# A transformer block on one core: an opening in a written order, query heads parted by DMA, and a planner that waits for copies

## The chip, the core and the metric

The kernel runs on one core of a Trainium2 chip. A core has five engines that run side by side and each take their instructions strictly in order: TensorE (PE, matrix products into PSUM), VectorE (DVE), ScalarE (ACT, here mostly exponentials), GpSimd (POOL) and SyncE (SP, which here only issues DMAs). PSUM has eight banks of 128 x 512 fp32 values. The metric is the device time of one execution in microseconds; smaller is better.

## The reference

One block of a transformer over 2048 tokens of width 512, with 32 heads of width 16 and a gated feed-forward layer of width 1792, in bfloat16:

```python
qkv = layernorm(x) @ wqkv                       # split into q, k, v: 32 heads of 16
p   = softmax(q @ k.T * 16 ** -0.5)             # per head, 2048 x 2048
h   = x + (p @ v) @ wo
g, u = layernorm(h) @ w_gate, layernorm(h) @ w_up
out = h + (sigmoid(g) * u) @ w_down
```

All 2048 x 2048 scores of each of 32 heads must be exponentiated. That is most of the work: 2048 units of 128 keys x 512 queries.

## The kernel before, in words

**Heads and tiles.** Keys lie transposed in `KT[p]`, 128 rows for eight heads of 16 rows each. A score product uses 32 rows (two heads) at a time, so that four row groups j work side by side in the array. To get one head out of two, the queries are kept twice: in `QT[2p]` the rows of the odd heads are zero, in `QT[2p+1]` those of the even heads. `mask` (128 x 2) has the ones and zeros for this, `maskz` the same times the scale of the scores. `QTb` is a second home for the first pair of chunk 1. A group g is one of the eight `QT` tiles: four heads, one for each j.

**Exponentials on two engines.** Scores fall into PSUM tiles of two or three units (L1110). ACT exponentiates most units (L1475, `pt`, `xnT`, `xb`, `pe`, `QTb` are only different homes of its results). DVE takes the other units by integer arithmetic on the bits of fp16 numbers: one pass out of PSUM (L1292), then two shifted copies of it, made mostly by GpSimd (L1313). The value product (L1268) then has three parts for such a unit in place of one, or two where DVE adds two of the parts first (L1337).

**Value products.** `Vaug` has per head 16 value columns and one column of 0.5, which gives the sum of the softmax; `Vaug2` is a weighted copy. The sums gather in PSUM bank 0 (`acc`), which must be cleared before its first use.

**The opening** (L200 to L515). `x` comes in four chunks of 512 rows; chunk 0 is loaded row tile by row tile (128 rows each). The path to the first scores is, per row tile i: statistics (`s`), with a correction (`f`) where ACT computed them, root (`q`), reciprocal (`r`), normalization (`a`), transpose on PE (`t`), copy out of PSUM (`e`), and products with the first 128 columns of the key and query weights (`p`, `w`=0 or 1). Then keys are copied to `KT[0]` (`kt`) and queries to `QT[0]` and `QT[1]` (`qt`, `qu`), in halves of 256 columns. A small list scheduler (L449 to L512) chooses at build time which of these tasks goes next on which engine, by a rank and by assumed times; `go` marks that the first scores may start. Matmuls on a constant tile keep PE warm meanwhile (`keep_warm`, L475). Constants (a ramp, the identity, the masks, the 0.5 columns) are made by GpSimd, DVE and ACT between these tasks.

**The planner.** After the opening, one long loop (L1394 on) walks over score tiles and writes the instructions of all engines in an order of its own. It keeps a clock per engine (`T`), assumed costs for each kind of work, and queues of jobs for DVE, ACT and GpSimd. Dense products (projections, output projection, the feed-forward layer of finished query chunks) and value products fill PE between score tiles; if nothing fits, `stir` (L678) issues a matmul whose result isn't used. `PLAN` is a table of a few hundred overrides found offline: the key 16n + step changes what PE does at a step of tile n, and steps 12, 14 and 15 steer whether DVE adds parts, which j DVE takes, and whether DVE takes a unit of this tile at all. Since each override shifts the clocks, all later decisions depend on it.

**The query projection** (`prep_q`, L768). Four dense products, one scaling copy out of PSUM into `qd` (L778), and then two `split_q` instructions on DVE (L327) which multiply `qd` by the two columns of `mask` into the two `QT` tiles. It runs 15 times: for each pair p of each chunk, without the first one that the opening does itself. All DMAs after the opening (feed-forward weights at L855, transposes of normalized rows at L593 and L837, residual rows, outputs) are issued by SyncE in the order in which the planner reaches them.

Of the kernel before, what the change touches and what calls it, by code (L numbers as in the profile page):

```python
# [22 lines left out]
PLAN = {176: 5, 239: 2, 367: 1, 383: 1, 414: 3, 432: 9, 480: 5, 492: 1, 496: 3, 512: 4, 561: 1, 592: 3, 593: 9, 606: 3, 609: 3, 736: 5, 751: 2, 780: 2, 785: 1, 796: 1, 800: 4, 831: 1, 844: 2, 849: 3, 894: 3, 897: 9, 914: 9, 928: 3, 960: 2, 976: 3, 1025: 2, 1040: 3, 1041: 5, 1052: 2, 1072: 3, 1088: 2, 1100: 2, 1104: 5, 1105: 3, 1120: 3, 1170: 1, 1233: 3, 1280: 3, 1328: 4, 1359: 2, 1392: 3, 1440: 2, 1486: 3, 1681: 1, 1824: 5, 1840: 9, 1872: 4, 1953: 3, 1982: 1, 2001: 3, 2080: 3, 2095: 2, 2129: 3, 2161: 3, 2162: 2, 2176: 4, 2222: 1, 2239: 2, 2256: 4, 2257: 9, 2274: 4, 2287: 2, 2350: 3, 2412: 1, 2430: 2, 2465: 9, 2479: 2, 2480: 9, 2512: 2, 2556: 2, 2560: 4, 2574: 2, 2588: 2, 2592: 5, 2608: 9, 2767: 1, 2818: 3, 2833: 9, 2849: 5, 2864: 3, 2908: 1, 2972: 2, 3020: 1, 3036: 1, 3056: 1, 3072: 3, 3169: 4, 3180: 2, 3184: 4, 3217: 2, 3234: 4, 3280: 4, 3360: 2, 3537: 2, 3617: 3, 3644: 2, 3681: 9, 3744: 3, 3756: 2, 3760: 3, 3820: 2, 3905: 4, 3938: 3, 3953: 3, 4066: 4, 4080: 3, 4081: 4, 4096: 2, 4112: 2, 4124: 1, 4129: 9, 4191: 2, 4204: 1, 4207: 2, 4225: 3, 4268: 2, 4284: 1, 4288: 2, 4337: 2, 4352: 3, 4398: 3, 4510: 2, 4526: 1, 4641: 4, 4700: 2, 4734: 3, 4737: 4, 4752: 9, 4754: 2, 4784: 4, 4802: 4, 4878: 3, 4880: 4, 4910: 2, 4924: 1, 4928: 1, 4930: 4, 5022: 2, 5058: 3, 5072: 4, 5090: 3, 5121: 4, 5164: 1, 5182: 3, 5185: 3, 5200: 3, 5201: 3, 5265: 4, 5280: 3, 5294: 1, 5308: 1, 5345: 2, 5359: 1, 5360: 9, 5378: 3, 5388: 1, 5424: 1, 5471: 1, 5488: 1, 5522: 2, 5553: 3, 5566: 3, 5600: 2, 5633: 4, 5650: 9, 5696: 2, 5712: 4, 5728: 4, 5742: 2, 5756: 2, 5760: 3, 5840: 2, 5906: 1, 5938: 3, 6082: 9, 6095: 2, 6096: 2, 6108: 2, 6140: 1, 6192: 3, 6194: 9, 6268: 1, 6274: 3, 6289: 4, 6319: 1, 6337: 5, 6384: 1, 6431: 2, 6432: 4, 6463: 2, 6464: 4, 6528: 3, 6544: 3, 6592: 1, 6607: 2, 6624: 1, 6641: 2, 6656: 2, 6687: 2, 6689: 9, 6753: 9, 6799: 1, 6832: 2, 6847: 2, 6865: 1, 6929: 2, 6972: 2, 6974: 1, 7024: 1, 7040: 3, 7106: 9, 7152: 5, 7154: 9, 7244: 2, 7248: 3, 7281: 3, 7296: 2, 7312: 1, 7376: 2, 7408: 9, 7410: 2, 7468: 1, 7504: 4, 7505: 2, 7520: 3, 7535: 2, 7553: 4, 7566: 3, 7570: 4, 7585: 3, 7596: 2, 7676: 1, 7681: 5, 7695: 2, 7728: 4, 7776: 3, 7793: 2, 7839: 2, 7852: 1, 7886: 2, 8016: 2, 8033: 2, 8063: 2, 8128: 2, 8209: 4, 8257: 9, 8290: 4, 8305: 9, 8338: 4, 8382: 2, 8432: 5, 8494: 3, 8529: 5, 8591: 2, 8609: 5, 8626: 2, 8706: 3, 8721: 4, 8768: 4, 8800: 4, 8848: 2, 8849: 5, 8860: 1, 8863: 2, 8881: 3, 8882: 4, 8895: 2, 8896: 3, 8897: 2, 8910: 3, 8927: 1, 8946: 4, 8961: 4, 9006: 1, 9024: 3, 9026: 9, 9054: 3, 9073: 2, 9116: 2, 9120: 3, 9137: 4, 9153: 2, 9249: 5, 9276: 2, 9358: 2, 9376: 3, 9377: 9, 9407: 1, 9408: 1, 9426: 9, 9457: 3, 9504: 2, 9518: 3, 9520: 4, 9584: 9, 9586: 4, 9600: 2, 9678: 1, 9697: 1, 9711: 2, 9727: 2, 9728: 1, 9762: 9, 9776: 4, 9792: 4, 9841: 9, 9854: 2, 9855: 2, 9857: 9, 9872: 3, 9900: 1, 9919: 2, 9932: 1, 9964: 2, 9968: 3, 10028: 2, 10032: 2, 10044: 2, 10047: 1, 10146: 2, 10160: 5, 10172: 1, 10176: 3, 10177: 3, 10210: 4, 10273: 4, 10284: 1, 10304: 3, 10334: 1, 10364: 2, 10380: 2, 10417: 9, 10433: 4, 10464: 1, 10556: 1, 10622: 1, 10624: 4, 10626: 9, 10636: 1, 10640: 4, 10690: 3, 10702: 2, 10705: 3, 10734: 3, 10754: 4, 10801: 3, 10802: 2, 10816: 2, 10848: 9, 10912: 1, 10913: 1}  # L23
# [121 lines left out]
def kernel(  # L145
# [103 lines left out]
    nc.vector.memset(eps_t[:], 1e-5)  # L249
    nc.scalar.activation(out=A0[:], in_=eps_t[:], func=ACT.Sqrt)  # L250
# [3 lines left out]
    nc.gpsimd.memset(power[:], -0.5)  # L254
    ramp = prep.tile([P, 2, 32], BF16, name="ramp")
    for k in range(32):
        nc.gpsimd.memset(ramp[:, 0, k:k + 1], float(k))
# [6 lines left out]
    def halves():  # L264
        nc.scalar.activation(out=Vaug[:, :, :, DH:VW], in_=fill[:].rearrange("p (t h o) -> p t h o", t=NT, o=1),
                             func=ACT.Copy, scale=0.5)

    def masks():
        nc.vector.tensor_reduce(out=mask[:], in_=ident_bf[:].rearrange("p (b a d) -> p a b d", a=2, d=DH),
                                axis=AX.XY, op=ALU.max)  # L270
        nc.vector.tensor_scalar(out=maskz[:], in0=mask[:], scalar1=ZS, scalar2=None, op0=ALU.mult)

# [57 lines left out]
    psp = main.enter_context(tc.tile_pool(name="psum", bufs=1, space=PSUM))  # L330
    PS = psp.tile([P, 8, QC], FP32, name="PS")
    free_banks = [5, 7, 6, 3, 2, 1, 0]
    held_banks = {}

    def bank0(key):
        b = held_banks[key] = free_banks.pop()
        return PS[:, b, :]

    def free0(key):
        free_banks.append(held_banks.pop(key))  # L340
# [7 lines left out]
    class Task:  # L348
        def __init__(self, name, deps, opts, bank=0, frees=0):
            self.name, self.deps, self.opts, self.bank, self.frees = name, deps, opts, bank, frees  # L350
            self.end = None
            tasks[name] = self

    def fixed(name, at):
        Task(name, [], []).end = at

    V, A, E = nc.vector, nc.scalar, nc.tensor

    ACT_STATS = {(0, 1)}

    def stats_task(c, i):
        src, mv = xb[c][:, i, :], mvs[c][:, i, :]

        def on_act():
# [6 lines left out]
        Task(("s", c, i), [("x", c, i)], [("A", 1650, on_act)] if (c, i) in ACT_STATS  # L371
             else [("D", 870, lambda: ln_stats(src, mv))])
        Task(("f", c, i), [("s", c, i)], [("D", 300, lambda: fix(c, i))] if (c, i) in ACT_STATS
             else [("N", 0, lambda: None)])
# [19 lines left out]
    def copy0(c, i, eng):  # L394
        eng(out=xnv[c][:, i], in_=buf["t", c, i])
        free0(("t", i))
# [7 lines left out]
    def keys0(half, act):  # L404
        cs = slice(half * 2 * P, (half + 1) * 2 * P)
        (A.copy if act else V.tensor_copy)(out=KT[0][:, cs], in_=buf[0][:, cs])
        if half:
            free0(0)

    def query0(half, a, act=False):  # L410
        cs = slice(half * 2 * P, (half + 1) * 2 * P)
# [5 lines left out]
        if half and a:  # L417
            free0(1)

    fixed("w0", 5000.0)  # L420
    for c in range(NQC):
        for i in range(TQ):
            fixed(("x", c, i), (3150.0 + 450 * (i // 2)) if c == 0 else 4800.0 + 2100 * c + 150 * i)
            stats_task(c, i)
# [1284 lines left out]
```

## Time and profile before

The median of three runs is 734.85 us (734.73 to 734.94); the profiled execution spans 733.3 us, and the clock granted to TensorE was 0.999 of full speed.

| what | busy us | share |
|---|---|---|
| PE | 712.8 | 97% |
| ACT | 703.1 | 96% |
| DVE | 663.3 | 90% |
| POOL | 421.8 | 58% |
| ACT exponentials out of PSUM into `pt`, the largest form | 469.9 | 479 instructions, 1099 ns each |
| DVE first pass of its exponentials (L1292) | 410.8 | 623 instructions |
| DVE query splits (L327) | 12.0 | 30 instructions |
| first scores on PE | | at 12.93 us |
| first exponentials on ACT | | at 13.36 us |

A busy share is an average over stages with different limits, so a table by stretches of time is needed beside it. In rows of groups, the columns are line, engine, operation, written tile <- read tiles, shapes, count, then busy time in us and mean ns of one, then idle time of the engine just before them. In an excerpt in order of time, each row begins with start and length in us, and a bracket tells how long the engine had been idle and what ended that. Matmuls of four row groups overlap, so the busy times of PE's groups can't be added up.

### The profile page before, as it was taken

The page shows a single profiled execution, that of the slowest core. Times are in us where ns is not written, and L with a number is a line of the kernel's source. Part 1 is how long each engine was busy: PE and PEld are TensorE (multiplying, and loading weights), DVE is VectorE, ACT ScalarE, POOL GpSimd, SP SyncE. Part 2 cuts the span into 40 slices and gives each one's busy share as a digit, 9 for nine tenths or more (in the row PEclk, how much of TensorE's full clock was granted, in tenths as well). Part 3 has the DMA queues.
Part 4 walks back from the last instruction along what each step waited for, and adds up shares of the span by engine and source line. Part 5 has one row for each costly group of instructions (what it writes and reads, how often), then busy time and mean ns, then how long its engine had stood idle before and what let it go on. Part 6 is the DMA issues. An engine that isn't in the chain of part 4 may idle for free.

```text
span 733.3 us, 26424 instructions
## 1 busy us (share of the span) xinstructions
PE 712.8 (97%) x11194; PEld 337.8 (46%) x11194; DVE 663.3 (90%) x1314; ACT 703.1 (96%) x787; POOL 421.8 (58%) x727
## 2 busy tenths in 40 slices
PE   7999999999999999999999999999999999999997
PEld 3222224443555445544545455445554455445564
DVE  6989999989999999999999899999999988999952
ACT  7999999999999999999999999999999999999962
POOL 2724667675665556656546656655654656656610
PEclk9999999999999999999999999999999999999999
DMA  7200005000223013220223023201322133012260
GB/s 244 49 11 2 1 1 175 2 3 2 74 75 87 11 26 101 83 57 25 59 66 84 22 68 102 66 25 31 100 62 52 38 89 117 17 45 78 84 175 18
DMA packets 80893, 44.49 MB, mean 61 GB/s; under 512 B 15489, under 2 KB 80769, under 8 KB 80769
## 3 DMA queue, kind: packets, MB, share of 16 engines
q1 hardware_dynamic: 80480, 42.48, 20.5%
q8 instruction: 89, 1.46, 0.8%
q10 hardware_dynamic: 288, 0.26, 0.1%
q14 instruction: 36, 0.29, 0.1%
HBM read 37.75 MB, written 2.10 MB: 54 GB/s over the span
## 4 chain that ended last, share of the span: by engine, by line
PE 55%; ACT 22%; DVE 17%; issue 3%; POOL 2%; DMA 0%; POOLq 0%; DVEq 0%; ACTq 0%
PE PS L1110 18%; PE PS L1268 15%; ACT pt L1475 15%; PE PS L847 9%; DVE J L1292 8%; PE PS L865 6%; ACT xnT L1475 2%; DVE J L1337 2%; POOL J L1313 2%; PE PS L314 2%; PE PS L319 2%; PE PS L790 1%; ACT th L877 1%; DVE st L274 1%; ACT xb L1475 1%
## 5 line engine op out<-in xcount | busy, mean ns | idle before, releaser
L1313 POOL INT64_ADD J<-J x658 | 403.7, 626 | 260.9 <-DVE J L1292 217.7
L1475 ACT ACTIVATE pt<-PS 128x1024 f16<-128x1024 f32 (+1 forms) x512 | 513.3, 1128 | 3.9 <-PE PS L1110 2.8
L1292 DVE TENSOR_SCALAR J<-PS 128x512 int16<-128x512 f32 x623 | 410.8, 678 | 22.3 <-PE PS L1110 16.5
L1110 PE MATMUL PS<-QT,KT 32*128 32x256 bf16 (+1 forms) x3712 | 264.4, 276 | 10.0 <-ACT pt L1475 6.4
L1268 PE MATMUL PS<-J,Vaug 128*17 128x256 f16 (+1 forms) x3218 | 226.8, 279 | 0.9 <-DVE xs L1176 0.3
L1268 PE MATMUL PS<-pt,Vaug 128*17 128x256 f16 (+1 forms) x2021 | 191.9, 279 | 0.0
L1110 PEld LDWEIGHTS <-KT 32*128 32x128 bf16 x3840 | 90.5, 92 | 204.6 <-issue 201.0
L1268 PEld LDWEIGHTS <-Vaug 128*17 128x17 bf16 x5871 | 132.2, 90 | 79.7 <-issue 74.5
L847 PE MATMUL PS<-xnT,wgu 128*128 128x256 bf16 x784 | 112.4, 275 | 0.7 <-DMA xnT<-hn 0.2
L1475 ACT ACTIVATE xnT<-PS 128x1024 f16<-128x1024 f32 (+1 forms) x88 | 96.3, 1131 | 0.0
L847 PEld LDWEIGHTS <-wgu 128*128 128x128 bf16 x784 | 64.5, 98 | 38.7 <-issue 33.0
L1337 DVE TENSOR_TENSOR J<-J 128x1024 f16<-128x1024 f16 (+1 forms) x97 | 67.8, 701 | 9.7 <-POOL J L1313 9.3
L865 PE MATMUL PS<-wd,hT 128*128 128x512 bf16 x196 | 56.7, 384 | 0.0
L1268 PE MATMUL PS<-xnT,Vaug 128*17 128x256 f16 x360 | 51.8, 273 | 0.0
L877 ACT ACTIVATE th<-PS 128x512 f32<-128x512 f32 (+1 forms) x63 | 39.1, 620 | 8.4 <-DVE hT L860 5.6
L1475 ACT ACTIVATE QTb<-PS 128x1024 f16<-128x1024 f32 x39 | 43.2, 1108 | 0.3 <-PE PS L1110 0.3
L919 DVE SCALAR_TENSOR_TENSOR hT<-th,PS 128x512 bf16<-128x512 f32 x49 | 33.2, 677 | 2.8 <-PE PS L847 2.8
L1475 ACT ACTIVATE xb<-PS 128x1024 f16<-128x1024 f32 (+2 forms) x29 | 29.9, 1093 | 0.3 <-PE PS L1110 0.3
L1176 DVE STREAM_TRANSPOSE xs<-PS 128x256 f32<-128x256 f32 (+1 forms) x60 | 27.4, 456 | 1.8 <-PE PS L1268 1.6
L1475 ACT ACTIVATE pe<-PS 128x1024 f16<-128x1024 f32 (+2 forms) x26 | 26.0, 1061 | 1.7 <-PE PS L1110 1.6
L1268 PE MATMUL PS<-QTb,Vaug 128*17 128x256 f16 x156 | 27.1, 274 | 0.0
L1147 DVE TENSOR_TENSOR o<-xs,rsum 128x128 bf16<-128x128 f32 (+1 forms) x60 | 24.2, 403 | 2.1
(126 smaller groups left out, 401.5 us busy)
## 6 DMA issues: line engine op xcount, KB each, us to landing
wgu<-in_B_w_gate_dram SPq DMA_DIRECT2D x49, 256.0 KB, 3.0
wgu<-in_B_w_up_dram SPq DMA_DIRECT2D x49, 256.0 KB, 3.4
out_dram<-ob SPq DMA_DIRECT2D x16, 128.0 KB, 1.7
wd<-in_B_w_down_dram SPq DMA_DIRECT2D x1, 1792.0 KB, 8.8
xr<-in_A_x_dram SPq DMA_DIRECT2D x14, 128.0 KB, 3.6
xb<-in_A_x_dram SPq DMA_DIRECT2D x6, 256.0 KB, 6.4
J<-in_B_w_gate_dram SPq DMA_DIRECT2D x4, 384.0 KB, 5.5
J<-in_B_w_up_dram SPq DMA_DIRECT2D x4, 384.0 KB, 6.3
```

What stands on the lines that cost most here:

```text
L847: nc.tensor.matmul(ps[:, 0:PARTS[r][2]].rearrange("p (i q) -> p i q", q=P), lhsT=w[:, d, :], rhs=hn_of(r)[:, :, d, :], start=(d == 0), sto ...
L865: nc.tensor.matmul(ps, lhsT=hT[:, f, i * P:(i + 1) * P], rhs=wd[:, f, :], start=(f == 0), stop=(f == FC - 1))
L877: nc.scalar.activation(out=th[:, 0:ps.shape[-1]], in_=ps, func=ACT.Tanh, scale=0.5)
L919: nc.vector.scalar_tensor_tensor(out=hT[:, f:f + k, 0:w], in0=th[f][:].rearrange("p (k n) -> p k n", k=k), scalar=1.0, in1=ps2.rearrange(" ...
L1110: nc.tensor.matmul(pss[:, ui, i * CW[qc]:(i + 1) * CW[qc]], lhsT=KT[g // 2][32 * j:32 * j + 32, k * P:(k + 1) * P], rhs=q[32 * j:32 * j + ...
L1147: nc.vector.tensor_tensor(out=o2[:, 0:w // 32, DH * a:DH * a + DH], in0=xs[:, 0:w // 32, 0:DH], in1=rec.to_broadcast([P, w // 32, DH]), op ...
L1176: j = dve(650 - ns[0], lambda: nc.vector.transpose(out=xs[:, 0:w // 32, :].rearrange("p b r -> p (b r)"), in_=src), LAST, st["xs"], pr=-1)
L1268: nc.tensor.matmul(dst[32 * j:32 * j + VW, 0:w], lhsT=un.v[:, kt * SPAN[qc] + i, h, :], rhs=un.ap[:, i * w:(i + 1) * w], start=clears and ...
L1292: nc.vector.tensor_scalar(out=J[:, 0, k, :], in0=src, scalar1=ZOFF, scalar2=float(-min(CHORDS)), op0=ALU.add, op1=ALU.max)
L1313: nc.gpsimd.int64_add(words(s), words(0), CHORDS[s - 1] * (1 + 2 ** 16 + 2 ** 32 + 2 ** 48))
L1337: nc.vector.tensor_tensor(out=f1, in0=f1, in1=J[:, 0, 0:k, :].bitcast(FP16), op=ALU.add)
L1475: ex = nc.scalar.activation(out=pt, in_=pss[:, 0:wa, :], func=ACT.Exp, scale=AS)
```

## The change

The change has five parts.

- **Opening.** The list scheduler is gone. `START` is a written order of the opening's tasks with their engines (A, D, P and the task's name), and each task's assumed cost is new. Banks are assigned by a table. ACT clears the accumulator's bank at the start, where DVE cleared it after the opening. The second query tile (`QT[1]`) and the second half of the keys are made after the first scores, the former by one instruction over 512 columns.
- **Constants.** The ramp is made by doubling on DVE, the 0.5 columns of `Vaug` by GpSimd, and the masks directly after the identity, all while `x` is being loaded.
- **Query heads by DMA.** GpSimd zeroes `QT[2]` to `QT[7]` and `QTb` once. `prep_q` then issues eight DMAs, each of 16 rows of `qd` to the same rows of the tile to which that head belongs. The other rows stay zero. The two `split_q` instructions go.
- **Clocks.** In the planner, scores wait for the copies of the keys and queries that they read, and value products for the copies of the values. The assumed times of DMAs and of GpSimd's library load change.
- **PLAN** is a new table, 360 entries for 356, six of them common to both. The key 16n + 12 with value 1 (DVE adds parts) occurs 42 times, before 25 times.

The diff, cut to its core:

```diff
+START = "As1 Ds0 Ds2 Aq0 Dr0 Da0 Pt0 Aq2 Df1 Ds3 Aq1 Ae0 Pp10 Dr2 Da2 Aq3 Aexps Dr1 Da1 Dr3 Da3 Pt2 De2 Pt1 Pp00 Pt3 Ae3 Pp12 De1 Pp01 Dkt0 Pp11 Dqt0 Pp13 Aqt1".split()
...
     nc.vector.memset(eps_t[:], 1e-5)
+    psp = main.enter_context(tc.tile_pool(name="psum", bufs=1, space=PSUM))
+    PS = psp.tile([P, 8, QC], FP32, name="PS")
+    acc = PS[:, 0, :]
+    nc.scalar.activation(out=acc, in_=eps_t[:].to_broadcast([P, QC]), func=ACT.Copy, scale=0.0)
     nc.scalar.activation(out=A0[:], in_=eps_t[:], func=ACT.Sqrt)
...
+    nc.gpsimd.memset(Vaug[:, :, :, DH:VW], 0.5)
+    for q in QT[2:] + [QTB]:
+        nc.gpsimd.memset(q[:], 0.0)
     ramp = prep.tile([P, 2, 32], BF16, name="ramp")
-    for k in range(32):
-        nc.gpsimd.memset(ramp[:, 0, k:k + 1], float(k))
+    nc.vector.memset(ramp[:, 0, 0:1], 0.0)
+    for k in (1, 2, 4, 8, 16):
+        nc.vector.tensor_scalar(out=ramp[:, 0, k:2 * k], in0=ramp[:, 0, 0:k], scalar1=float(k), scalar2=None,
+                                op0=ALU.add)
...
-    def halves():
-        nc.scalar.activation(out=Vaug[:, :, :, DH:VW], in_=fill[:].rearrange("p (t h o) -> p t h o", t=NT, o=1),
-                             func=ACT.Copy, scale=0.5)
...
+    masks()
...
+    for word in START:
+        t, eng = tasks[word[1:]], word[0]
+        ns, fn = t.opts[eng]
+        at = max([free[eng]] + [seen(d, eng) for d in t.deps])
         if eng == "P":
-            keep_warm(start)
-            start = max(start, free["P"])
-        t.end = start + ns
...
-    acc = PS[:, 0, :]
-    nc.vector.memset(acc, 0.0)
+    go = max([free["P"]] + [seen(n, "P") for n in ("qt0", "qt1", "kt0", "exps")])
+    keep_warm(go)
...
-    DMA_T = 3000.0
+    DMA_Q = 2700.0
+    DMA_T = 2700.0
...
-        job = pm_out(dve(603, lambda: nc.vector.tensor_scalar(
-            out=qd[:], in0=ps, scalar1=ZS, scalar2=None, op0=ALU.mult), st["mark"]))
-        done["q", qc, p] = [dve(262, lambda a=a: split_q(dst, a, qd), job) for a in range(2)]
+
+        def scale():
+            nc.vector.tensor_scalar(out=qd[:], in0=ps, scalar1=ZS, scalar2=None, op0=ALU.mult)
+            for k in range(2 * QC // 128):
+                rows = slice(DH * k, DH * k + DH)
+                nc.sync.dma_start(out=dst[k % 2][rows], in_=qd[rows])
+        job = pm_out(dve(603, scale, st["mark"]))
+        done["q", qc, p] = [Later(job, DMA_Q)]
...
-        for u in tiles[n]:
-            need(u)
+        at = max([need(u) for u in tiles[n]], default=0.0)
...
+        T["P"] = max(T["P"], at + LAT)
         T["P"] = max(T["P"], ex_end.get(n - 2, 0.0) + LAT)
...
-                and un.end + LAT <= T["P"] + loose]
+                and un.end + LAT <= T["P"] + loose and values_in(un, loose)]
...
-            T["G"] += 9000.0
+            T["G"] += 6000.0
...
     pss_n = {0: scores(0)}
+    for i in (2, 3):
+        proj0(0, i)
+    pe_time("dense", 560.0)
+    query0(None, 1)
+    T["D"] = max(T["D"] + 660.0, T["P"] + DRAIN + LAT) + 430.0
+    keys0(1, False)
```

## The prediction

> **What bounds the kernel now.** I read the shares of the engines first, then the table by stretches of time, then the waits, then the opening in order of time, and last the rows that the change touches.
>
> ```profile
> PE 712.8 (97%) x11194; PEld 337.8 (46%) x11194; DVE 663.3 (90%) x1314; ACT 703.1 (96%) x787; POOL 421.8 (58%) x727
> ```
>
> Three engines are nearly full over the span, so an average can't say which sets the time. The table by stretches can (PE, weight loads, DVE, ACT, POOL, each with its count; then clock and DMA):
>
> ```profile
> 13.36:40.00 26.64, 24.63 (x146) 7.39 (x146) 23.83 (x55) 24.45 (x27) 16.27 (x30) 1.00 0.31 74
> 40.00:110.00 70.00, 69.65 (x637) 19.27 (x636) 65.50 (x115) 69.09 (x74) 38.06 (x64) 1.00 0.01 1
> 110.00:190.00 80.00, 74.43 (x1341) 34.17 (x1337) 73.68 (x146) 79.41 (x86) 52.77 (x87) 1.00 0.16 45
> 190.00:700.00 510.00, 506.12 (x8806) 253.65 (x8804) 479.80 (x937) 507.63 (x559) 312.53 (x508) 1.00 0.22 62
> ```
>
> From 40 us on ACT is busy 99 to 99.5%. PE is as full from 190 to 700 (99.2%), but from 110 to 190 it idles 5.6 us, and 7.7 us of its work there is the stir matmul of L678, which computes nothing. DVE is 92 to 94% full. So ACT binds from 110 to 190, ACT and PE together after it, and DVE time is worth what it takes off those two. Waits inside the body are small already: PE waited 6.4 us in all for exponentials, and 1.1 us once for a copy of keys (L757).
>
> The opening is a chain. Columns: start, length, engine, line, what.
>
> ```profile
> 3.76 0.69 DVE L274 BATCH_NORM_STATS2 st<-xb 128x6 f32<-128x512 bf16 x1 [0.40 <-DMA xb<-in_A_x_dram]
> 4.94 0.28 ACT L384 ACTIVATE rstd<-mv,eps_t 128x1 f32<-128x1 f32 x1
> 6.51 0.25 DVE L427 RECIPROCAL rstd<-rstd 128x1 f32<-128x1 f32 x3
> 7.04 1.36 DVE L388 TENSOR_SCALAR xn<-xb,mv,rstd 128x512 bf16<-128x512 bf16 x4
> 8.65 0.28 DVE L269 TENSOR_REDUCE mask<-ident_bf 128x2 f32<-128x128 bf16 x1
> 12.93 0.40 PE L1110 MATMUL PS<-QT,KT 32*128 32x512 bf16 x4
> 13.36 1.02 ACT L1475 ACTIVATE pt<-PS 128x1024 f16<-128x1024 f32 x1
> ```
>
> The root of the first row tile is out at 5.22, but its reciprocal runs at 6.51 and its normalization at 7.04, behind the statistics of all four tiles. That is an order, not a need. The masks stand at 8.65 among the copies, where the transposes wait for them. The chain of waits after this stays on DVE (statistics, Vaug, copies) until 28.6 us.
>
> The rows of the query split and of the queue that would take it over:
>
> ```profile
> L327 DVE TENSOR_SCALAR QT<-qd,mask 128x512 bf16<-128x512 bf16 x28 | 11.3, 419 | 0.0
> L327 DVE TENSOR_SCALAR QTb<-qd,mask x2: 341/343/345, 54.2 to 55.9; 128x512 bf16<-128x512 bf16 x2
> SPq L855 <- PE PS L1110: 288.9, 44, 14.7
> ```
>
> Thirty splits take 11.3 + 0.7 = 12.0 us of DVE. The last line is the SyncE queue: it stood 288.9 us at gate loads waiting for their buffer, so it has room, but it is in order.
>
> **What the Trainium skill says.** "SBUF — State Buffer", Who interferes with whom: a two-port tensor_scalar and GpSimd lock each other out for a whole instruction. The splits agree, 312 ns at least and 732 at most beside GpSimd's adds; so removing them also spares GpSimd waits. "Perfetto Trace Analysis", Per-instruction lifecycle: the queue's recorded span of a DMA is waiting for the generator and making descriptors, the transfer comes after. The trace has 0.37 to 0.51 us per issue whatever the size, and 2.4 us to landing for a transpose inside SBUF. "ScalarE: Activation LUTs", Table sets: copy and identity lie in every table. Agrees: Identity (L366) and Copy (L395) ran without a load of their own; a load is 1283 ns.
>
> **The change, part by part.** *Opening.* I put the written order on the durations of the trace, and pass from engine to engine in 0.02 to 0.05 us, as the trace does. ACT now also clears the accumulator bank ahead of its first load: about 0.6 us (L1600, 597 ns, same size), so its statistics of tile 1 start at 3.75 instead of 3.56. DVE: statistics 0 and 2 from 3.76 to 5.46; root 0 on ACT ends at 5.42; reciprocal and normalization 0 end at 5.98 (before: 7.44). Transposes 0.40 to 6.42; ACT root of tile 1, then copy 0.59 to 7.14; first query product to 7.6. DVE meanwhile: fix 0.4, statistics 3, then three reciprocals and normalizations, to 8.42. PE: transposes of 2, 1, 3 to 9.1; DVE copies 2 and 1 to 9.14; ACT loads the Exp table by 8.9 and copies 3 to 9.7. Products end about 9.8 (keys of half 0) and 10.4 (queries of half 1); keys to KT to 10.24, queries to QT to 10.7 on DVE and 10.86 on ACT. First scores: 10.9 by this count. I take 11.2, because PE fills gaps with 0.2 to 0.4 us warming matmuls and the new GpSimd fills (below) can hold a normalization once. Gain 12.93 - 11.2 = 1.7 us. DVE's chain moves alike: second query half 0.67, keys of half 1 after two more products, at about 12.4 free for chunk 1 instead of 14.16, also 1.7. Because the chain then stays on DVE to 28.6 us, the gain is kept. Bounds: 1.0 (lockouts, a transfer of weights that lands late) to 2.2.
>
> *Constants.* The masks (0.28 + 0.17), the bank's clearing (0.48) and the halves of Vaug (2.41 on ACT at 10.35) leave the opening. The masks are in the chain above; the clearing was 0.48 of DVE's chain and is in the 1.7; the halves lay beside PE and only delayed the second half of keys: nothing. The ramp on DVE, five dependent adds of 0.13 to 0.24, then transpose and compares (0.9), ends near 3.2, before x: nothing. GpSimd now fills Vaug, six QT and QTb: by its own fill (524 ns for 512) some 5 us, done by about 6.5; it was idle until 15.91. Nothing, but for the lockout above.
>
> *Query splits.* Removes 12.0 us of DVE. Adds 15 x 8 = 120 DMAs on SyncE's queue, at 0.37 to 0.5 us of issue each: 3 to 4 us for one query tile, landing some 2.4 us later, so 5.5 to 6.5 us after the copy; the planner counts 2.7. Who waits? The trace has the splits of QTb at 54 and its first scores at 67.1, those of the next pair at 67 and scores still on QTb at 98; the later ones were due groups ahead. So no scores wait. The price of the new wait is what is queued behind it: gate loads come 5 to 10 us apart and land 3.4 us after issue; 3 to 4 us in front can make PE wait about 1 us where two meet. In the trace such meetings are few, since a query projection takes the place of a gate product. I take 0.2 us in all, from 0 to 4.
>
> What are the 12.0 us worth? A unit of exponentials moved from ACT to DVE costs DVE 659 (L1292: 410.8/623) + 109 (L1337 shared: 67.8/623) = 0.77 us and frees 470/479/2 = 0.49 us of ACT. It costs PE 1.7 more value products: by the chain of waits 24 of these matmuls take 0.78 us and 40 take 1.21, so 0.027 each, 0.054 a unit, 0.09 in all. One add (L1337, 744 ns) saves PE two units, 0.11 us. Eight splits lie before 190 us, where ACT binds and PE has room: 8 x 0.40 = 3.2 us, 4.2 units, 2.0 us of ACT. Twenty-two lie where both bind: 8.8 us spent so that ACT and PE fall alike is about 2 units and 10 adds, 1.0 us. Upper end 3.0; lower end 0, if the time only becomes idle DVE. The new plan forces 42 adds where the old one forced 25, which is the second way of spending it. I take three quarters, 2.3.
>
> *The clocks.* Waiting for copies of keys and values in the planner changes order only. The waits it could mend sum to under 2 us, mostly the 1.1 at 28.6. I count 0.1, to even out the queue's 0.2.
>
> Sum: 734.85 - 1.7 - 2.3 + 0.1 = 730.85, say **730.8 us**.
>
> **The rivals.** *Opening only.* DVE's time turns into idle time, because ACT and PE are both full and the new order is no better than the old one: 734.85 - 1.7 = 733.1. For: PE at 99.2% from 190 us. Against: the stir matmuls and PE's idle 5.6 us before it. *More.* The whole plan is new, and a planner whose clocks know the copies loses fewer of ACT's 3 and PE's 5.6 idle us: opening 2.2, DVE 3.0, 2 more of those: 727.6. Against: ACT has only 0.5% idle. *Slower.* The SyncE queue runs late before gate loads or transposes (15 x 0.3 = 4 us), and the plan, made for other durations than the chip's (2.7 us for the eight copies), puts products where PE waits; or ACT's early Copy brings a load of its own (1.28 on the chain), eating most of the opening: 734.85 - 0.5 + 2 = 736.4. For: waits were tiny before, an equilibrium that a new order can lose. Against: the queue has gaps and nothing critical uses the copies at once.
>
> **How the numbers follow.** Forecast 0.55, opening only 0.17, more 0.12, slower 0.16. Faster by over 0.2% (under 733.4): all of the first and third, most of the second: 0.79. Slower over 736.3: half of the last and a little more: 0.12. The rest, 0.09, is same. The range takes the forecast's bounds, opening only, and the nearer part of the two others: 727.4 to 734.8; about 0.2 is left out.
>
> **What the profile after would show.** First scores near 11.2 and normalization 0 near 5.6: the opening is right; a second table load before 5 us or a normalization over 0.6 us: wrong there. No L327, DVE busier by adds or units instead of idle; ACT's busy sum lower by 2 us or more from 110 to 190: the DVE step is right; equal ACT sums mean the rival. PE waits on wgu, or scores on a DMA of QT, over 1 us in sum: the queue was under-priced. The prediction fails most easily by the plan itself, which fixes the order of 700 tiles and which no row of this profile prices.

## The result

The changed kernel takes 741.06 us (median of four runs, 740.45 to 741.30) against 734.89 (734.73 to 734.99) for the kernel before: a ratio of 1.0083 with an interval of 1.0065 to 1.0100. It is 6.2 us slower, where 4.1 us faster was forecast. The profiled executions span 739.5 and 733.3 us, the same difference.

The changed kernel's profile, read where the prediction read the kernel before. First the shares of the engines and the two rows in which the new plan shows (line, engine, operation, tiles, count, then busy us and mean ns, then idle time before and what ended it):

```profile
PE 715.7 (97%) x11144; PEld 337.6 (46%) x11144; DVE 674.0 (91%) x1311; ACT 701.7 (95%) x787; POOL 435.8 (59%) x711
...
L1252 DVE TENSOR_SCALAR J<-PS 128x512 int16<-128x512 f32 x627 | 411.7, 678 | 15.5 <-PE PS L1060 12.2
L1297 DVE TENSOR_TENSOR J<-J 128x1024 f16<-128x1024 f16 (+1 forms) x117 | 83.6, 714 | 13.0 <-POOL J L1273 12.1
```

DVE lost the 12.0 us of splits and is 10.7 us busier than before. The plan gave it four more units (627 for 623) and twenty more adds (117 for 97, +15.8 us). The rest, 6 us, is in the opening, the next view to read (start, length, engine, line, what):

```profile
0.93 6.86 DVE L267 TENSOR_SCALAR ramp<-ramp 128x1 bf16<-128x1 bf16 x5
1.25 2.27 POOL L261 MEMSET Vaug<- 128x512 bf16 x1
1.66 1.28 ACT L255 ACT_TABLE_LOAD   x1 [1.66 <-PEq L1659]
3.12 3.13 POOL L263 MEMSET QT<- 128x512 bf16 x6
3.56 1.28 ACT L256 ACT_TABLE_LOAD   x1
6.19 0.95 POOL L263 MEMSET QTb<- 128x1024 bf16 x1
9.20 0.69 DVE L283 BATCH_NORM_STATS2 st<-xb 128x6 f32<-128x512 bf16 x1
10.98 0.41 DVE L387 TENSOR_SCALAR xn<-xb,mv,rstd 128x512 bf16<-128x512 bf16 x1
11.45 0.61 PE L317 MATMUL PS<-ident_bf,xn 128*128 128x128 bf16 x4 [4.60 <-DVE xn L387]
19.07 1.02 ACT L1441 ACTIVATE pt<-PS 128x1024 f16<-128x1024 f32 x1 [0.50 <-PE PS L1060]
```

Three things are to be seen. The five adds of the ramp, forecast at 0.13 to 0.24 us each, take 6.86 us, and the statistics start at 9.20 where they started at 3.76. ACT loads two tables, at 1.66 and 3.56. And from the first normalization to the first exponential takes 8.1 us, 1.6 us longer than in a kernel of the experiments below with the same written order (6.5 us, the first one). In all, the first exponential comes at 19.07 instead of 13.36: 5.7 us later. The ramp's first two adds by themselves tell which instruction it was:

```profile
0.93 0.16 DVE L267 TENSOR_SCALAR ramp<-ramp 128x1 bf16<-128x1 bf16 x1
1.12 6.05 DVE L267 TENSOR_SCALAR ramp<-ramp 128x2 bf16<-128x2 bf16 x1
```

The second add, of two elements a partition, is recorded with 6.05 us. It ends at 7.17, just after GpSimd's last fill, which began at 6.19 and took 0.95. The first add, of one element, took 0.16.

The table by stretches of time (PE, weight loads, DVE, ACT, POOL, each with its count; then clock, DMA):

```profile
9.96:16.79 6.83, 5.34 (x39) 4.24 (x40) 4.65 (x17) 3.73 (x8) 0.00 (x0) 0.50 0.98 310
...
40.00:110.00 70.00, 69.01 (x587) 18.55 (x588) 64.16 (x111) 67.83 (x71) 36.78 (x60) 1.00 0.05 12
110.00:190.00 80.00, 74.32 (x1305) 32.44 (x1300) 74.58 (x139) 78.20 (x86) 55.88 (x90) 1.00 0.15 43
```

The clock granted to TensorE was 0.50 from 9.96 to 16.79 us, just when the chain of the opening ran through it. In the body ACT is busy 1.2 us less than before from 40 to 110, and again from 110 to 190. The forecast took such a drop as the sign of units moved to DVE, but DVE took only four more over the whole kernel. Most of it is idle time: from 40 to 190 us ACT's exponentials into `pt` waited 3.0 us for scores, where they waited 1.1 us before. From the first exponential to the end it takes 739.5 - 19.07 = 720.4 us, before 733.3 - 13.36 = 719.9.

The last views are SyncE's queue and the waits on it:

```profile
L727 SPq DMA_DIRECT2D QT<-qd x112: 507/587/1714, 74.4 to 568.1; - x112
```
```profile
264.54 4.93 SPq L727 DMA_DIRECT2D QT<-qd  x8
269.57 4.68 SPq L786 DMA_TRANSPOSE xnT<-hn  x2
```
```profile
PE PS L796 <- DMA xnT<-hn: 1.9, 3, 1.0
```

Eight issues take 4.9 us, not 3 to 4. No scores waited for the query copies (weight loads of gate products did, 0.4 us in all), but PE waited 1.9 us for transposed rows, whose DMAs stand in the same queue.

### The profile page after: what moved, and what is told of

The parts are those of the page before. It is cut to its first block, busy times and chain, and to the rows that moved or that the text cites. A ratio compares the mean times of both kernels' runs of the same rounds, so it can differ in the third digit from the quotient of the medians.

```text
span 739.5 us, 26526 instructions
## 1 busy us (share of the span) xinstructions
PE 715.7 (97%) x11144; PEld 337.6 (46%) x11144; DVE 674.0 (91%) x1311; ACT 701.7 (95%) x787; POOL 435.8 (59%) x711
## 4 chain that ended last, share of the span: by engine, by line
PE 61%; DVE 18%; ACT 13%; issue 4%; DMA 2%; POOL 1%; DVEq 0%; ACTq 0%; POOLq 0%; SPq 0%
PE PS L1060 20%; PE PS L1228 16%; PE PS L796 12%; ACT pt L1441 10%; DVE J L1252 9%; PE PS L814 4%; PE PS L328 2%; PE PS L739 1%; DVE J L1297 1%; ACT xnT L1441 1%; POOL J L1273 1%; PE PS L323 1%; DMA xnT<-hn 1%; DVE hn L784 1%; DVE ramp L267 1%
## 5 line engine op out<-in xcount | busy, mean ns | idle before, releaser
L1273 POOL INT64_ADD J<-J x666 | 412.7, 632 | 252.4 <-DVE J L1252 208.2
L1252 DVE TENSOR_SCALAR J<-PS 128x512 int16<-128x512 f32 x627 | 411.7, 678 | 15.5 <-PE PS L1060 12.2
L1228 PE MATMUL PS<-J,Vaug 128*17 128x256 f16 (+1 forms) x3171 | 224.0, 279 | 1.1 <-DVE J L1297 0.4
L1228 PE MATMUL PS<-pt,Vaug 128*17 128x256 f16 (+1 forms) x2026 | 195.8, 279 | 0.0
L1228 PEld LDWEIGHTS <-Vaug 128*17 128x17 bf16 x5817 | 130.2, 90 | 79.4 <-issue 74.6
L1297 DVE TENSOR_TENSOR J<-J 128x1024 f16<-128x1024 f16 (+1 forms) x117 | 83.6, 714 | 13.0 <-POOL J L1273 12.1
L1441 ACT ACTIVATE xnT<-PS 128x1024 f16<-128x1024 f32 (+1 forms) x87 | 93.7, 1124 | 0.1
L1228 PE MATMUL PS<-xnT,Vaug 128*17 128x256 f16 x354 | 50.3, 274 | 0.0
L1441 ACT ACTIVATE QTb<-PS 128x1024 f16<-128x1024 f32 x41 | 45.4, 1106 | 0.0
L1441 ACT ACTIVATE xb<-PS 128x1024 f16<-128x1024 f32 (+1 forms) x27 | 26.2, 1001 | 0.5 <-issue 0.2
L1098 DVE TENSOR_TENSOR o<-xs,rsum 128x128 bf16<-128x128 f32 (+1 forms) x60 | 23.1, 385 | 2.1
L1441 ACT ACTIVATE pe<-PS 128x1024 f16<-128x1024 f32 (+1 forms) x24 | 24.6, 1077 | 0.2 <-PE PS L1060 0.2
```

What stands on the lines that cost most here:

```text
L1098: nc.vector.tensor_tensor(out=o2[:, 0:w // 32, DH * a:DH * a + DH], in0=xs[:, 0:w // 32, 0:DH], in1=rec.to_broadcast([P, w // 32, DH]), op ...
L1228: nc.tensor.matmul(dst[32 * j:32 * j + VW, 0:w], lhsT=un.v[:, kt * SPAN[qc] + i, h, :], rhs=un.ap[:, i * w:(i + 1) * w], start=clears and ...
L1252: nc.vector.tensor_scalar(out=J[:, 0, k, :], in0=src, scalar1=ZOFF, scalar2=float(-min(CHORDS)), op0=ALU.add, op1=ALU.max)
L1273: nc.gpsimd.int64_add(words(s), words(0), CHORDS[s - 1] * (1 + 2 ** 16 + 2 ** 32 + 2 ** 48))
L1297: nc.vector.tensor_tensor(out=f1, in0=f1, in1=J[:, 0, 0:k, :].bitcast(FP16), op=ALU.add)
L1441: ex = nc.scalar.activation(out=pt, in_=pss[:, 0:wa, :], func=ACT.Exp, scale=AS)
```

## The experiments

The theory at the outset: the opening lost what it lost because the ramp's adds were locked out by the run of GpSimd fills; all else moved little. The rivals were the second table load (a loss on ACT's side of the chain), the new order of the body, and the DMAs.

**The ramp in another form.** The fills stay as they are; the ramp's adds and the scaling of the mask become tensor_tensor, with a second input made by small memsets.

```diff
-        nc.vector.tensor_scalar(out=ramp[:, 0, k:2 * k], in0=ramp[:, 0, 0:k], scalar1=float(k), scalar2=None,
-                                op0=ALU.add)
...
+        nc.vector.tensor_tensor(out=ramp[:, 0, k:2 * k], in0=ramp[:, 0, 0:k], in1=step[:, k:2 * k], op=ALU.add)
...
-        nc.vector.tensor_scalar(out=maskz[:], in0=mask[:], scalar1=ZS, scalar2=None, op0=ALU.mult)
+        nc.vector.tensor_tensor(out=maskz[:], in0=mask[:], in1=zs_t, op=ALU.mult)
```

> The changed kernel with the same constants made by VectorE in another form: the ramp's adds and the scaled mask are tensor_tensor with a second operand in SBUF in place of tensor_scalar. GpSimd's fills stay as they are. Lockout theory (a two-port tensor_scalar of VectorE waits until GpSimd's run of fills is over): the adds take under 0.25 us each, statistics start at 4 to 4.5 us instead of 9.2; the first normalization, itself a two-port tensor_scalar, still can't run before the fills end at 7.1 and starts at 7.2; first scores at 12.8 to 13.3 instead of 18.6, and 735 to 736 us against 741. Rival (VectorE waits for GpSimd by a dependency or is slow in short dependent adds): the ramp ends near 7.7 again and the time stays at 741.

Measured: ratio to the kernel before 1.0024 (1.0012 to 1.0037), span 734.3 us. Its opening, with the same fills at the same times:

```profile
1.20 0.75 DVE L272 TENSOR_TENSOR ramp<-ramp,KT 128x2 bf16<-128x2 bf16 x4
3.12 3.13 POOL L263 MEMSET QT<- 128x512 bf16 x6
3.47 0.69 DVE L287 BATCH_NORM_STATS2 st<-xb 128x6 f32<-128x512 bf16 x1
3.54 1.28 ACT L256 ACT_TABLE_LOAD   x1
6.31 0.46 ACT L387 ACTIVATE rstd<-mv,eps_t 128x1 f32<-128x1 f32 x2
6.62 0.16 DVE L423 RECIPROCAL rstd<-rstd 128x1 f32<-128x1 f32 x1 [1.44 <-ACT rstd L387]
6.82 0.47 DVE L391 TENSOR_SCALAR xn<-xb,mv,rstd 128x512 bf16<-128x512 bf16 x1
13.32 1.02 ACT L1445 ACTIVATE pt<-PS 128x1024 f16<-128x1024 f32 x1 [0.50 <-PE PS L1064]
```

The adds take 0.16 us each beside the same fills, and the first exponential moves from 19.07 to 13.32. With the third experiment, where the form stays and the fills go, this settles the lockout: the delay needs both, and 5.75 us of the opening hang on the form of a few tiny instructions. The expectation also had the first normalization, a tensor_scalar too, wait for the fills until 7.2. It didn't: it began at 6.82, 0.3 us before the last fill ended, and took 0.47 us where the other three took 0.41. The first normalization comes 4.16 us earlier (6.82 for 10.98); the other 1.59 us lie between it and the first exponential, and the clock granted here stays at 1.00. The kernel is still no faster than before, for DVE now waits 1.44 us for ACT's root, which stands behind the second table load.

**One table load alone.** The changed kernel with Sqrt ahead of the clearing Copy, all else as it is.

```diff
-    nc.scalar.activation(out=acc, in_=eps_t[:].to_broadcast([P, QC]), func=ACT.Copy, scale=0.0)
     nc.scalar.activation(out=A0[:], in_=eps_t[:], func=ACT.Sqrt)
+    nc.scalar.activation(out=acc, in_=eps_t[:].to_broadcast([P, QC]), func=ACT.Copy, scale=0.0)
```

> The changed kernel with nothing but the square root ahead of the clearing of the bank: one table load instead of two. VectorE's statistics start at 9.2 in the changed kernel, ACT had waited 3.7 us for them, so a load hidden there is worth nothing: 741 within 0.3. If the second load was on the path: 739.7.

Measured: 1.0058 (1.0034 to 1.0083), first exponential at 18.75. The swap does spare the load, and it is worth nothing here. ACT reaches its root early and waits for DVE, and the root runs at 10.14 as it did with two loads:

```profile
10.14 0.29 ACT L383 ACTIVATE rstd<-mv,eps_t 128x1 f32<-128x1 f32 x1 [5.12 <-DVE mv L286]
```

So the second load is not what made the kernel slower, though it is what held up the kernel of the first experiment. The first exponential still came 0.32 us earlier, and the reason is the clock. Here the half clock ran from 9.12 to 15.95, 0.84 us ahead of the changed kernel's. From 9.2 us on DVE and ACT are at the same times in both, to 0.01 us, until twelve products for keys and queries. The first row is the changed kernel's, the others are from here:

```profile
15.69 1.36 PE L399 MATMUL PS<-xnT,w 128*128 128x128 bf16 x12
15.70 0.95 PE L399 MATMUL PS<-xnT,w 128*128 128x128 bf16 x12
9.12:15.95 6.83, 4.49 (x31) 3.39 (x32) 5.46 (x19) 3.15 (x8) 0.00 (x0) 0.50 1.00 332
```

The five executions differ by the clock too. Granted 0.999 over the whole execution, this kernel took 737.5 and 738.0 us; granted 0.994 to 0.995, as the changed kernel was each time, it took 740.6 to 741.8. So the drop goes with some 3 us. No trace of the two shorter executions is kept, so it isn't known whether their ramp was held as long.

**Fills taken out of the opening.** Here the ramp keeps its form, and GpSimd's fills of the query tiles move to after the early normalizations and the first query projections (`zero(n)` fills the next n tiles, `QTB` first). The 0.5 columns follow right after the opening.

```diff
-    nc.gpsimd.memset(Vaug[:, :, :, DH:VW], 0.5)
-    for q in QT[2:] + [QTB]:
-        nc.gpsimd.memset(q[:], 0.0)
...
         def scale():
+            zero(1 if (qc, p) == (1, 0) else len(ZERO))
```

> The changed kernel, with GpSimd's early fills taken away: the zeros of the query tiles are written one tile at a time after the early normalizations (from about 40 us), and the 0.5 columns of Vaug after the opening, from the finished query tile times zero. The order of everything else stays. Lockout theory: the ramp of tensor_scalars is done by 2 us, statistics start at 3.8; the second table load of ACT now shows, since its statistics of tile 1 begin at 4.96 as before: first normalization near 6.9, first scores 12.0 to 12.6, time 734.5 to 735.5. Rival (the ramp is slow by itself): no change, 741. Rival (the opening's delay is made up later, and the body is what is slower): 739 to 741 in spite of an early start.

The second kernel does the same and has Sqrt ahead of Copy as well:

> As e2_late_fills, and ACT takes the square root ahead of the clearing of the bank, so that one table load is enough. If the opening is the whole loss and the body is worth nothing: ACT's statistics start near 3.8, first normalization at 5.6, first scores at 11.0 to 11.6, time 741 minus 7.5, about 733.5. If the freed VectorE time was worth the forecast 2.3 us in the body: about 731. If the new order of the body is itself slower: 735 or more.

Measured: 1.0040 (1.0026 to 1.0054) and 1.0032 (1.0025 to 1.0039), both slower than expected. The openings do what they should: the ramp takes 1.03 us in the first, the first exponential comes at 13.29 in the first and 11.94 in the second, so a table load that is exposed is worth 1.35 us. The loss comes later and is of my making. In the second kernel:

```profile
34.22 0.95 POOL L464 MEMSET QTb<- 128x1024 bf16 x1
35.11 1.91 POOL L464 MEMSET QT<- 128x512 bf16 x4
42.89 1.20 POOL L1279 INT64_ADD J<-J  x2 [5.87 <-DVE Vaug L330]
45.47 0.37 PE L1066 MATMUL PS<-QT,KT 32*128 32x512 bf16 x1 [1.28 <-DVE J L1258]
```

GpSimd's first 64-bit adds start 5.87 us after its last work of another kind. Fills put in front push that start back, PE stands 1.28 us for the parts that DVE and GpSimd had to make, and the clock is 0.50 from 47.03 to 53.86. Two later fills between such adds (44.04 to 45.00 us) brought no such gap. The clock doesn't fall each time: this trace is one of five executions in twenty that were granted 0.994 to 0.995 and took 739.2 to 739.7 us; the others took 736.1 to 738.2. Even those are slower than the kernel before. These two kernels show the opening's part but not a clean time.

**Zeros by DMA.** GpSimd fills only `QTb`; six DMAs copy zeros from it. With the ramp as tensor_tensor, the 0.5 columns after the opening, and Sqrt ahead of Copy, nothing of the change's intent is lost.

```diff
-    nc.gpsimd.memset(Vaug[:, :, :, DH:VW], 0.5)
-    for q in QT[2:] + [QTB]:
-        nc.gpsimd.memset(q[:], 0.0)
+    nc.gpsimd.memset(QTB[:], 0.0)
+    for q in QT[2:]:
+        nc.sync.dma_start(out=q[:], in_=QTB[:, 0, :])
...
```

> The changed kernel with its opening mended: GpSimd fills only QTb early, six DMAs copy these zeros to the query tiles, the 0.5 columns of Vaug come from GpSimd after the opening, the ramp and the scaled mask are made by tensor_tensor, and ACT takes the root ahead of the clearing (one table load). GpSimd's library load is not pushed back, as it was by the late fills. Theory (the whole loss lies in the opening, the body is as long as before's): first exponentials at 11.9, and 720.4 to 721 us from there to the end as in the changed kernel and in e1: span 732.3 to 733, time 734 to 734.5. Rival (the body can use an early start, and the freed VectorE time is worth 2 us): 732. Rival (the body holds the end by itself, for instance by a queue or a transfer at a fixed time): 736 or more.

Measured: 0.9988 (0.9981 to 0.9995), span 732.9. First normalization, scores and exponential:

```profile
5.51 0.41 DVE L391 TENSOR_SCALAR xn<-xb,mv,rstd 128x512 bf16<-128x512 bf16 x1
11.54 0.39 PE L1066 MATMUL PS<-QT,KT 32*128 32x512 bf16 x2
11.97 2.85 ACT L1447 ACTIVATE pt<-PS 128x1024 f16<-128x1024 f32 x3 [0.50 <-PE PS L1066]
```

This is the opening as forecast: normalization near 5.6, first scores near 11.2. But the kernel is 0.9 us faster than before although its opening alone gains 1.4. From the first exponential to the end it takes 720.9 us, as the changed kernel does (720.4). So the new body returns nothing for the 12 us of DVE.

**What the splits are worth, in both orders.** First the mended kernel (the one with zeros by DMA) with the DVE splits in place of the eight DMAs, at the same order of work:

```diff
             for k in range(2 * QC // 128):
                 rows = slice(DH * k, DH * k + DH)
-                nc.sync.dma_start(out=dst[k % 2][rows], in_=qd[rows])
+                pass
+            for a in range(2):
+                split_q(dst, a, qd)
```

> As e5_zeros_by_dma, and the query heads are parted by the two VectorE instructions again, at the place where the eight DMAs were issued, with the planner's order unchanged. It puts some 12 us of work on VectorE and takes 120 DMAs from SyncE. If VectorE's time in this order is worth what the prediction said (2.3 to 3 us for 12): 2 to 3 us longer than e5. If ACT and PE hide it: within 0.5 us of e5. If VectorE is on the path in this order: 5 to 12 us longer. If the DMAs in front of transposes cost more than they free: shorter than e5 by up to 2 us.

Measured: 1.0109 (1.0092 to 1.0126), that is 9.0 us over the mended kernel (743.29 and 734.31). The waits of PE for units that DVE made, 0.2 and 0.4 us in all in the mended kernel, show part of how:

```profile
PE PS L1068 <- DVE J L1260: 2.1, 7, 0.5
PE PS L1236 <- DVE J L1305: 1.5, 3, 0.7
```

Then the other way about: the kernel before, with its own opening, plan and clocks, and DMAs for the splits. GpSimd zeroes the tiles after its own ramp, in which DVE has no part.

```diff
+    for q in QT[2:] + [QTB]:
+        nc.gpsimd.memset(q[:], 0.0)
...
-        job = pm_out(dve(603, lambda: nc.vector.tensor_scalar(
-            out=qd[:], in0=ps, scalar1=ZS, scalar2=None, op0=ALU.mult), st["mark"]))
-        done["q", qc, p] = [dve(262, lambda a=a: split_q(dst, a, qd), job) for a in range(2)]
+
+        def scale():
+            nc.vector.tensor_scalar(out=qd[:], in0=ps, scalar1=ZS, scalar2=None, op0=ALU.mult)
+            for k in range(2 * QC // 128):
+                rows = slice(DH * k, DH * k + DH)
+                nc.sync.dma_start(out=dst[k % 2][rows], in_=qd[rows])
+        job = pm_out(dve(603, scale, st["mark"]))
+        done["q", qc, p] = [dve(262, lambda: None, job) for a in range(2)]
```

> The kernel before with one part of the change alone: eight DMAs in place of the two splits, into tiles that GpSimd zeroes right after its ramp (2.4 to 6.6 us, when VectorE runs no two-port instruction). The planner's clocks and the order stay as if the splits were there. If 12 us of VectorE are worth the forecast 2.3 us at a fixed order: 732.6. If they only become idle VectorE time, because PE and ACT are full: 734.5 to 735. If the DMAs' 5 us on SyncE hold up gate loads and transposes: 736 or more.

Measured: 0.9971 (0.9960 to 0.9983), 2.0 us faster (733.28 and 735.31). The moments at which groups of heads end show when it was gained: against the kernel before, the difference is 0.1 us through 261 us, 1.2 at about 347, and 2.0 at about 515. DVE's idle time waiting for scores rose from 16.5 to 23.1 us:

```profile
DVE J L1299 <- PE PS L1117: 23.1, 85, 1.1
```

So of 12 us of DVE the time falls by 2.0, and more than half of what was set free becomes waiting. Put into an order made without it, for which the planner set no time aside, the same work costs 9.0: three quarters of itself. A later experiment takes DVE work out of that same order and gains little. So the worth of DVE time bends like a knee at the point where the order was made.

**The plan and the clocks.** Four kernels part the order of the body from the rest. The first two have an empty `PLAN`: the mended kernel, and the kernel before.

```diff
+PLAN = {}
```

> As e5_zeros_by_dma, with an empty PLAN: the planner's own rules and new clocks alone. To be set beside the kernel before with an empty PLAN, which is to follow. If the new clocks and the freed VectorE time make a better order by themselves, it is under that one by 3 us or more; if the body is a tie, within 3 us. Against e5 it shows what the overrides are worth: 8 to 20 us.

> The kernel before with an empty PLAN. Its distance to 734.9 is what the old overrides were worth; the new ones were worth 10.8 us (e8 against e5). If the old table was the better searched one, this lies 13 us or more above the kernel before, at 748 or more; if both searches gained alike, 745 to 747.

Measured: 1.0138 (1.0121 to 1.0155) and 1.0166 (1.0150 to 1.0182). The overrides are worth 745.08 - 734.31 = 10.8 us in the new kernel and 747.15 - 735.04 = 12.1 in the old one. Both planners need their table. The old table does a little more, but not by more than the noise.

The third kernel has the mended opening and the DMAs, and for the rest the old body: old `PLAN`, clocks and order after the opening.

```diff
-    T = {e: max(0.0, free[e] - go) for e in free}
+    T = {"P": 100.0, "A": 600.0, "D": 710.0, "G": 0.0}
...
-        T["P"] = max(T["P"], at + LAT)
...
-                and un.end + LAT <= T["P"] + loose and values_in(un, loose)]
+                and un.end + LAT <= T["P"] + loose]
```

> The mended opening of e5 in front of the body of e7: the order, PLAN and clocks of the kernel before, with DMAs in place of the splits. From the first scores on every engine has the order of e7. It differs from e5 in the body's order alone. If the new body order costs time (theory): first exponentials at 11.95, then 718.4 us to the end as in e7: span 730.3, time 732.0, about 2.3 us under e5. If the difference between e5 and e7 comes from how the opening hands over to the body: equal to e5, 734.3. If the early start is lost again in the early pass: 733.3, as e7.

Measured: **0.9962 (0.9948 to 0.9975)**, 732.08 us against 735.04.

```profile
11.89 1.02 ACT L1444 ACTIVATE pt<-PS 128x1024 f16<-128x1024 f32 x1 [0.50 <-PE PS L1066]
```

It is the only kernel here that gains on both counts, and it beats both the kernel before and the changed one. Its first exponential is at 11.89 (before 13.36: 1.5 us), and from there to the end it takes 718.4 us (before 719.9: 1.5 us). The mended kernel differs from it in the order of the body alone, with the same opening to 0.1 us, and takes 720.9: the new order costs about 2.5 us by the spans, 1.9 by the ratios. (In the changed kernel itself it is 2.0 by the spans: 720.4 against 718.4.)

The fourth is this kernel with `PLAN = {}`.

> As e10_old_body_new_opening with an empty PLAN: old clocks, freed VectorE time that the planner doesn't know of. It differs from e8 in the clocks alone. If the new clocks make the better order by themselves: 3 us or more above e8 (745.1), so 748 or more. If they don't: within 3 us or below, and then the loss of the new body lies in the clocks or in chance, and not only in the overrides.

Measured: 1.0129 (1.0113 to 1.0144), beside 1.0138 for the new clocks without a plan. The intervals overlap; by themselves the new clocks can't be told to be better or worse. On this opening and with these DMAs the old table is worth 744.31 - 732.08 = 12.2 us, the new one 10.8 on its clocks, which is not clear of the noise either. So the loss belongs to the new order as a whole, the table together with the clocks that it was found on; no run parts the two.

**Fewer adds.** Is it the twenty extra adds? The mended kernel with every sixth of DVE's adds left out; the parts of the softmax that these would have added are not computed.

```diff
-                nc.vector.tensor_tensor(out=f1, in0=f1, in1=J[:, 0, 0:k, :].bitcast(FP16), op=ALU.add)
+                st["adds"] = st.get("adds", 0) + 1
+                if st["adds"] % 6:
+                    nc.vector.tensor_tensor(out=f1, in0=f1, in1=J[:, 0, 0:k, :].bitcast(FP16), op=ALU.add)
```

> As e5_zeros_by_dma, with every sixth add of two parts (19 of the 117) left out: its sum lacks one part there, so part of the softmax is not computed. The order and the work of all other engines stay; VectorE has 13 to 14 us less work, about the 97 adds of the kernel before. If VectorE sets the length of the new body (e6 cost 9 us for 12): 4 to 9 us under e5, so 725 to 730. If the new order spent VectorE's freed time only until it was as full as ACT and PE, and these set the length: 0 to 2 us under e5, so 732.5 to 734.5; then what the body lost is in the waits on ACT, PE and transfers.

Measured: 0.9968 (0.9956 to 0.9981), 1.6 us below the mended kernel (732.72 and 734.31). That is for 19 adds, 19 x 0.72 = 13.7 us of DVE. So the adds explain at most about this part of the body's loss (every sixth went, not the twenty that are new, and PE was not given the products back that they spare), and 0.12 us per us of DVE is again the flat side of the knee. A wait that the old order hardly has is still in the list, PE on transposed rows behind SyncE's queue (1.7 us here, 2.4 in the mended kernel).

## Why the prediction was wrong

The sum over the profiled executions: opening +5.7, DVE relief in the old order -1.5 (719.9 to 718.4 from the first exponential on), new order of the body +2.0 (718.4 to 720.4), together +6.2, which is what was measured. The prediction had -1.7, -2.3, nothing for the order and +0.1 for queue and clocks. (These add up to 730.95 us; its 730.85 leaves out the last 0.1.)

**Constants: this step failed.** It said of the ramp "ends near 3.2, before x: nothing", and of the fills "Nothing, but for the lockout above". The lockout was in my hands: the Trainium skill, "SBUF — State Buffer", Who interferes with whom, was cited in the prediction, and the ramp's adds are of the kind it names (tensor_scalar out of SBUF into SBUF). The runs show that the delay takes this form and the fills together; that a shared port is the reason is what the page says. I asked only whether it would hold a normalization, and for one instruction. It held the ramp, and for a whole run of back-to-back fills: 6.05 us. The same section says that an instruction with two inputs in SBUF does not contend with GpSimd work that only writes, which the first experiment confirms at 0.16 us an add. Of the 5.75 us, 4.16 are the delay itself. The other 1.59 go to the clock: PE ran out of warming matmuls, idled 4.6 us for the first normalization, and was granted 0.50 from 9.96 to 16.79. The second experiment supports this: with the half clock ending 0.84 us earlier, the first exponential came 0.32 us earlier, all else at the same times. But no trace has the late normalization with a warm PE, so the 1.59 as a whole is argued. The skill's "TensorE: Matmul & The Clock Gate", Part 1, gives half the clock after an idle window of about 3.4 us. The 4.6 us agree with that. The kernel with late fills and one load doesn't: it lost the clock at 47.03 after PE had stood idle for only 1.28 us, so these runs don't show how much idle time it takes.

**ACT clears the bank.** The forecast took 0.6 us for it and left a second load to the rivals. The load did come, at 3.56. "ScalarE: Activation LUTs", Table sets, has copy in every set, and I had read this as no load; but a Copy that comes first brought a load of its own, and Sqrt another. Hidden behind DVE's delay it cost nothing; exposed, with the late fills, it cost 1.35.

**The opening's order** was right, once the lockout and the second load are taken out: first scores at 11.54 and 11.46 for a forecast of 11.2, first exponential 1.4 to 1.5 us earlier for 1.7.

**Query splits.** The size came out right by luck; the mechanism and the place were wrong. The relief came to 2.0 us in the kernel before's own order, for 2.3 forecast. But the 2.0 us that I had assigned to the eight splits before 190 us (of 3.0, before I took three quarters) came to nothing (0.1 by 261 us), and the later ones, put at 1.0, gave 1.9. ACT at 99% there did not get the freed time, since no unit moves from ACT to DVE while the order stays the same; what DVE gained was waiting. My conversion into moved units needs a plan that moves them. Nor did GpSimd gain the waits that I said the splits cost it: its 64-bit adds took 403.7 us before and 402.9 without the splits.

**The queue** was under-priced at 0.37 to 0.5 us an issue: 0.59, so 4.9 us for eight. The waits that I named as its sign didn't come: scores never waited for the copies, and gate loads held up PE's weight loads by 0.2 us. What came is a wait that only the rival "slower" named: PE waited 1.9 us on the transposes behind them. The old order with the same DMAs has only 0.4 us of it, on a weight load, and the kernel before has 0.2. So the DMAs cost this only together with the new order.

**The new order of the body.** I priced it at nothing but warned that "the plan itself" could fail most easily. It cost 2.0 us in the changed kernel and 2.5 in the mended one, set against the old order with the same DMAs. Its DVE spends 15.8 us more on adds, and PE is spared 54 value products in all, by the prediction's estimate 54 x 0.027 = 1.5 us. Leaving out 13.7 us of adds gave 1.6 us, so the adds are at most about that much of the 2.5; waits on transposes (2.4 us in the mended kernel) may be the rest. I did not take these waits away, so that share stays open. The planner's clocks are not shown to matter by themselves.

The rival "slower" held in its direction. Of its causes the second load came and cost nothing here, PE's wait on transposes came with 1.9 us, and the new order cost 2.0 in all; none was the main one. At 736.4 us it was 4.7 us short, because it lacked the lockout.

## What to carry to other kernels

When work moves to GpSimd, list every DVE instruction that falls into its run, the tiniest too, and ask of each whether it can be locked out; its length in a quiet profile says nothing. A chain that an engine serves in order turns one such instruction into a delay of everything after it, here of statistics, normalization and then the clock. And a table of overrides found for one kernel is a change by itself: run the old table with the new parts before judging either, as here the parts were worth 3.0 us with the old table and its clocks, and the new ones cost about 2 of that (1.9 by the ratios, 2.5 by the spans).

## What the runs showed of the hardware

- A tensor_scalar of two elements a partition, SBUF to SBUF in bf16, took 6.05 us beside an unbroken run of eight GpSimd fills and ended when the run was over: it did not get in between two of them. The add of one element before it took 0.16 beside another fill, and a tensor_tensor took 0.16 beside the same ones.
- The first activation of a kernel decides a table load even if it is a Copy: two loads of 1.28 us where Sqrt first needs one.
- GpSimd starts the first of its 64-bit adds 5.8 to 6.0 us after its last other work in every kernel looked at (5.83 before, 5.93 after, 5.79 and 5.87 with late fills, 5.95 in the mended kernel). Work put in front moves that start back. Fills between later adds brought no such gap.
- A fall of the granted clock to 0.50 lasted 6.83 us in each of the three traces that have one in the middle of the work: twice after PE had idled 4.6 to 5.0 us, once after 1.28 us.
- SyncE needs 0.59 us to issue a DMA of 16 rows inside SBUF, and the data lands 1.8 us later.
